# Output products of five FFN groups by a 2x2x2 Strassen scheme

## The chip, the cores and the metric

The kernel runs on one core of a Trainium2 chip. The core has a matrix engine (TensorE, PE in the profile), which multiplies a stationary operand of up to 128x128, loaded beforehand (PEld), with a moving operand of up to 512 columns and writes into PSUM; three engines for elementwise work (VectorE or DVE, ScalarE or ACT, GpSimd or POOL); and SyncE (SP), which in this kernel only issues DMAs. Each engine runs its own instructions in order, and semaphores order them between engines. The metric is the device time of one execution in microseconds (us), as the median of several runs.

## The reference, cut to what matters

```python
f = 1.0 / (1.0 + np.exp(-f_logit))                       # (4, 8, 768, 48): batch, head, time, feature
for t in range(S):
    state = f[:, :, t, :, None] * state + np.einsum('bhd,bhe->bhde', k[:, :, t], v[:, :, t])
    y[:, :, t] = np.einsum('bhd,bhde->bhe', q[:, :, t], state)
x = y.transpose(0, 2, 1, 3).reshape(3072, 384)
h = np.maximum(np.maximum(x @ w1, x @ w2), x @ w3)       # w1, w2, w3: (384, 768)
out = h @ w_out                                          # w_out: (768, 384)
```

A gated linear recurrence per head makes 3072 token rows of 384 features. A maxout FFN takes them to 768 and back to 384. Everything is float32 (the weights arrive as 64-bit floats and are converted on the chip).

## The kernel before, in words

The 3072 tokens are cut into 24 tiles of 128 (`NU`, index `u`: two batches by 64 time steps). Four tiles are one FFN group of `TOK` = 512 tokens (`GRP` = 4), so there are six groups, numbered g = 0 to 5 in the code.

*Attention.* For each tile, `sigmoids`, `scan`, `after`, `before` and `carry` prepare gates, decayed keys `kh`, decayed queries `qh` and the carried state; from the ninth tile on, `kh` (L328), `qh` (L339) and the carried `state` (L345) are GpSimd's. `pairs` (L380) multiplies keys with queries, `values` (L399, with `sums`, L424) applies the result to v and makes the new state, and `finish` (L470) adds what the state gives. ACT then copies y to the tile `heads` (L476, three copies). `pack` (L491) moves `heads` into `xT`, the transposed input of the FFN group, by ten DMAs: the eight heads have 48 rows each, and two of them cross a border between rows of 128. `pack(0, 2)` moves three tiles of a group together, `pack(3, 3)` the fourth. All ten are issued on SP, except at the very end, where SP and ACT take five each.

*FFN.* The first group runs `ffn_first`. During it, w1 is subtracted from w2 and w3 (`apart`), w1 is transposed (`turn`) and multiplied with w_out (`linear`); the product `w_lin` (384x384) lies in w1's place. With it the later groups use max(x w1, x w2, x w3) = x w1 + max(0, x(w2 - w1), x(w3 - w1)): `ffn(g, xT)` makes, for each of the six blocks `j` of 128 hidden rows, two products of 512 tokens (`product`, L511, three matmuls each, one for each `kt` of the 128-row blocks of `xT`). ACT applies Relu to the first (L612), VectorE takes the maximum with the second and writes `hm[:, j, :]` (L614). Then `outputs` makes one token tile of 128 at a time: three matmuls with `w_lin` (L528) and six with `w_out` (L532), all of 384 columns, into one PSUM buffer `p`; ACT copies it to `o` (L537), and `store` DMAs (L542) write two halves of 64 rows.

*The order.* It is written out by hand. The FFN is a queue of generators (`pending`), and each `yield` reports the nominal time of the matmuls just issued, `COLUMN` = 4/2.4 ns for each column. `fill(ns)` pulls parts from the queue until their reported time has used up `ns`; what is used too much or too little is carried on. From u = 4 on, every tile does: fill, `finish(u - 1)` and the packs, `pairs(u)`, loads and the next tile's sigmoids and scan, fill, `after` and `before` of the next tile, fill, `values(u)`, fill, loads, fill: five fills of `PART` = 2740 ns. `pack(3, 3)` and the start of the next `ffn` are both at the tiles u = 8, 12, 16, 20, and after the loop for the last group. What the group before has left in the queue at that point is issued before the next group's products.

*Buffers.* PSUM: two `p` buffers (`ps_f`), two `tr` buffers (`ps_tr`: transposes of the first eight tiles and the range test at the end), one each for `a` and `y`. In SBUF the weights are loaded as 64-bit words into `raw` buffers (12 of them). From u = 9 on they are loaded a second time, two pieces for each tile (`check_load`, L258), and ACT tests their range (`check_range`, L267 to L270). `o` has three buffers and serves the first tiles' x as well.

Of the kernel before, what the change touches and what calls it, by code (L numbers as in the profile page):

```python
# [9 lines left out]
FP32 = mybir.dt.float32  # L10
I32 = mybir.dt.int32
U32 = mybir.dt.uint32
AF = mybir.ActivationFunctionType
ALU = mybir.AluOpType
# [32 lines left out]
C = 64  # L47
# [8 lines left out]
def kernel(  # L56
# [12 lines left out]
    nc = tc.nc  # L69
# [3 lines left out]
    UT = 2 * C  # L73
# [16 lines left out]
    def fast():  # L90
        ctx = ExitStack()
        with ctx:
# [100 lines left out]
            pieces = [(w_in[i][:, :, j * 128:(j + 1) * 128], src[:, j * 128:(j + 1) * 128])  # L193
                      for j in range(NJ) for i, src in enumerate((moe_w1, moe_w2, moe_w3))]
            pieces += [(w_out[:, j:j + 1, :], moe_w_out[j * 128:(j + 1) * 128, :]) for j in range(NJ)]
            RAW = 12
            PIECE = NK * 128
            raw, raw_next = {}, []

            def load_weights(count, done=0, queue=nc.sync):  # L200

                for n in range(len(raw_next), min(len(raw_next) + count, done + RAW, len(pieces))):
                    raw_next.append(n)
                    dst, src = pieces[n]
                    a = dst.shape[1]
                    if src.dtype != FP32:
                        raw[n] = work.tile([128, 2 * PIECE], U32, name="raw", bufs=RAW)
                        dst, src = raw[n].rearrange("p (a c) -> p a c", a=a), src.bitcast(U32)
                    queue.dma_start(out=dst, in_=src.rearrange("(a p) c -> p a c", a=a))

# [42 lines left out]
            def check_load(n):  # L253
                src = pieces[n][1]
                if src.dtype != FP32:
                    raw[n] = work.tile([128, 2 * PIECE], U32, name="raw", bufs=RAW)
                    a = pieces[n][0].shape[1]
                    nc.sync.dma_start(out=raw[n].rearrange("p (a c) -> p a c", a=a),  # L258
                                      in_=src.bitcast(U32).rearrange("(a p) c -> p a c", a=a))
# [173 lines left out]

            heads = keep.tile([128, HP, TOK], FP32, name="heads")

            def y_by_tokens(u):

                d = ready[u]
                y = d["y"]
                if u >= 2:  # L440

                    new = states[u % 2][:, 0, 0:1]
                    nc.tensor.matmul(ps_f.tile([1, 1], FP32, name="p"), lhsT=new, rhs=new, start=True, stop=True)
                    st = d["state"].rearrange("p (a h) d -> p a h d", a=2)
                    for hp in range(HP):
                        for par, a in FOUR:
                            r = slice(par * DP, par * DP + D)
                            nc.tensor.matmul(y[a * C:(a + 1) * C, par, hp * D:(hp + 1) * D], lhsT=d["qh"][r, a, hp, :],
                                             rhs=st[r, a, hp, :], start=False, stop=(hp == HP - 1), skip_group_check=True)
                x = work.tile([UT, DM], FP32, name="o", bufs=3)  # L450
                nc.scalar.copy(x.rearrange("t (hp par d) -> t par hp d", hp=HP, par=2),
                               y[:, :, 0:HP * D].rearrange("t par (hp d) -> t par hp d", d=D))
                d["x"] = x
# [67 lines left out]
            def new_top(w):  # L521
                return work.tile([128, TOK], FP32, name="top")[:, 0:w]

            def outputs(g, hm, i, xT=None):
                p = ps_f.tile([128, TOK], FP32, name="p")
                if g:
                    for kt in range(NK):
                        nc.tensor.matmul(p[:, 0:DM], lhsT=xT[:, kt, i * UT:(i + 1) * UT], rhs=w_lin[:, kt, :],  # L528
                                         start=(kt == 0), stop=False)
                    yield NK * DM * COLUMN  # L530
                for j in range(NJ):
                    nc.tensor.matmul(p[:, 0:DM], lhsT=hm[:, j, i * UT:(i + 1) * UT], rhs=w_out[:, j, :],  # L532
                                     start=(g == 0 and j == 0), stop=(j == NJ - 1))
                    if j == NJ // 2 - 1:
                        yield NJ // 2 * DM * COLUMN
                o = work.tile([UT, DM], FP32, name="o", bufs=3)
                nc.scalar.copy(o, p[:, 0:DM])  # L537
                c, bp = divmod(g * GRP + i, 2)
                for a in range(2):
                    t0 = (2 * bp + a) * S + c * C  # L540
                    last = g * GRP + i == NU - 1 and a
                    (nc.scalar if last else nc.sync).dma_start(out=out[t0:t0 + C, :], in_=o[a * C:(a + 1) * C, :])  # L542
                yield NJ // 2 * DM * COLUMN

            def apart(j):

# [25 lines left out]
            def ffn_first(xT):  # L572
                hm = new_hm()
                steps = [(j, slice(n * HALF, (n + 1) * HALF)) for n in range(2) for j in range(J_HALF)]
                steps += [(j, slice(0, TOK)) for j in range(J_HALF, NJ)]
                done, n_step = 1, 0
                for j, t in steps:
                    w = t.stop - t.start
                    for i in range(3):
                        p = yield from product(0, xT, j, i, t)  # L580
                        if i == 0:
                            top = new_top(w)
                            nc.scalar.copy(top, p)
                        else:
                            nc.vector.tensor_tensor(hm[:, j, t] if i == 2 else top, p, top, op=ALU.max)
                        n_step += 1
                        ahead = n_step + 1 if n_step <= 6 else 7 + (n_step - 6) * 5 // 6 if n_step <= 12 else 12 + (n_step - 12) * 6 // 5
                        for r in range(done, min(ahead, len(pieces))):
                            if r + 2 < len(pieces):
                                round_begin(r + 2)  # L590
                            if r + 1 < len(pieces):
                                round_end(r + 1)
                            done = r + 1
                        load_weights(2, done)
                        yield (1 if w == TOK else NK) * w * COLUMN
                for i in range(GRP):
                    for j in range(i * NJ // GRP, (i + 1) * NJ // GRP):
                        apart(j)
                    yield from outputs(0, hm, i)
                    for j in range(i * NJ // GRP, (i + 1) * NJ // GRP):  # L600
                        yield from turn(j)
                for a in range(NK):
                    yield from linear(a)

            def ffn(g, xT):
                hm = new_hm()
                for j in range(NJ):
                    for i in (1, 2):
# [3 lines left out]
                            nc.scalar.activation(top, p, AF.Relu)  # L612
                        else:
                            nc.vector.tensor_tensor(hm[:, j, :], p, top, op=ALU.max)  # L614
                        yield TOK * COLUMN
                for i in range(GRP):
                    yield from outputs(g, hm, i, xT)

            pending = []

# [423 lines left out]
```

## Time and profile before

| what | value |
|---|---|
| median of 3 runs | 457.15 us (457.14 to 458.05) |
| the profiled execution, its own time | 457.98 us |
| its span from first to last instruction | 456.2 us |
| TensorE matmuls of the products, L511 | 504 records, 212.8 us busy |
| of the outputs, L532 and L528 | 288 and 120 records, 99.3 and 42.4 us busy |
| VectorE maximum `hm`, L614, 128x512 | 30, mean 681 ns |
| ACT copy `o`, L537, 128x384 | 24, mean 477 ns |
| GpSimd `kh`, `qh`, `state` (L328, L339, L345) | mean 1960, 1176, 857 ns |
| DMA `raw` (384 KB), `xT` (24 KB), `out` (96 KB) | 5.5, 1.9, 2.2 us from issue to landing |

How to read it: the span is one execution as the hardware profiler saw it, on one core. Busy time is the union of an engine's instructions. A float32 matmul shows as two records, one for each pass, and each has its own weight load. The recorded duration of a matmul includes the way through the pipeline, so records overlap: the spacing of their starts is what counts. The timeline merges neighbouring records of a kind and gives their number (x6), and in brackets how long the engine had been idle and who ended that. A line marked SPq or ACTq is the issuing of DMAs on that queue.

### The profile page before, as it was taken

What the parts mean: (1) busy time and instruction counts of PE and PEld (TensorE: products, weight loads), DVE (VectorE), ACT (ScalarE), POOL (GpSimd) and SP (SyncE); (2) the same over time, 40 slices, a digit from 0 to 9 for tenths busy, and PEclk for the clock granted to TensorE, in tenths of its full rate; (3) what the DMA queues carried; (4) which work ended last, traced back from release to release, by engine and by line L of the source; (5) the groups of instructions that cost most, each with busy time, mean ns of one, the idle gap of its engine ahead of it and who ended that gap; (6) DMA issues with size and microseconds to landing.
All of it is one profiled execution on the core that took longest, in us unless ns stands there. A gap on an engine that the chain in (4) does not pass through costs nothing.

```text
span 456.2 us, 10209 instructions
## 1 busy us (share of the span) xinstructions
PE 432.9 (95%) x4062; PEld 244.1 (54%) x4062; DVE 253.4 (56%) x510; ACT 150.1 (33%) x350; POOL 103.9 (23%) x125
## 2 busy tenths in 40 slices
PE   4989999999999999999999999999989999999995
PEld 3777655556554456554456654455544455544553
DVE  6976757556858569357779557759456520011100
ACT  2434757403312214414414524504324331111000
POOL 2153654403033033032033023023032120000000
PEclk9999999999999999999999999999999999999999
DMA  8889997202547733647763557643746003100011
GB/s 169 213 245 299 259 205 89 36 19 71 94 66 88 133 93 72 147 78 146 92 164 77 147 104 131 98 142 72 165 78 124 2 0 88 45 9 0 4 35 37
DMA packets 177140, 47.13 MB, mean 103 GB/s; under 512 B 154816, under 2 KB 175552, under 8 KB 177088
## 3 DMA queue, kind: packets, MB, share of 16 engines
q1 hardware_dynamic: 173616, 45.64, 47.6%
q10 hardware_dynamic: 3472, 0.79, 0.8%
q8 instruction: 33, 0.54, 0.5%
q14 instruction: 19, 0.16, 0.1%
HBM read 37.75 MB, written 4.72 MB: 93 GB/s over the span
## 4 chain that ended last, share of the span: by engine, by line
PE 84%; DVE 5%; ACT 4%; DMA 4%; issue 2%; SPq 1%; POOL 0%; ACTq 0%; DVEq 0%
PE p L511 42%; PE p L532 18%; PE p L528 7%; PE y L470 3%; PE p L565 3%; PE y L399 2%; PE y L424 2%; PE a L380 2%; DVE r L317 2%; DMA raw<-in_moe_w_out_dram 2%; ACT heads L476 1%; PE tr L279 1%; DMA xT<-heads 1%; ACT sig L299 1%; PE y L395 1%
## 5 line engine op out<-in xcount | busy, mean ns | idle before, releaser
L511 PE MATMUL p<-xT,w_in 128*128 128x512 f32 (+1 forms) x504 | 212.8, 569 | 7.5 <-ACT top L612 2.8
L511 PEld LDWEIGHTS p<-xT,w_in 128*128 128x128 f32 x504 | 92.0, 190 | 104.2 <-issue 85.2
L532 PE MATMUL p<-w_out,hm 128*128 128x384 f32 x288 | 99.3, 491 | 1.3 <-ACT w_in L558 1.0
L532 PEld LDWEIGHTS p<-w_out,hm 128*128 128x128 f32 x288 | 53.6, 190 | 37.1 <-ACT w_in L558 1.3
L370 DVE STREAM_TRANSPOSE ks<-kh 32x128 f32<-32x128 f32 x224 | 67.7, 302 | 3.5
L614 DVE TENSOR_TENSOR hm<-p,top 128x512 f32<-128x512 f32 x30 | 20.4, 681 | 80.9 <-PE p L511 80.5
L327 POOL COPY ends<-r 128x8 f32<-128x8 f32 x24 | 6.7, 279 | 187.0 <-DVE r L317 187.0
L612 ACT ACTIVATE top<-p 128x512 f32<-128x512 f32 x30 | 17.8, 594 | 91.9 <-PE p L511 91.9
L383 DVE TENSOR_TENSOR at<-a,mask 128x512 f32<-128x512 f32 x24 | 16.6, 692 | 48.8 <-PE a L380 48.8
L528 PE MATMUL p<-w_in,xT 128*128 128x384 f32 x120 | 42.4, 489 | 0.0
L537 ACT COPY o<-p 128x384 f32<-128x384 f32 x24 | 11.4, 477 | 93.6 <-PE p L532 90.1
L476 ACT COPY heads<-y 64x256 f32<-64x256 f32 (+1 forms) x60 | 22.1, 369 | 54.9 <-PE y L470 45.5
L328 POOL TENSOR_TENSOR kh<-kt,r 128x512 f32<-128x512 f32 x16 | 31.4, 1960 | 35.4 <-DVE kt L284 33.2
L317 DVE TENSOR_TENSOR_SCAN r<-gate,from_one 128x520 f32<-128x520 f32 x24 | 29.8, 1241 | 6.6 <-ACT gate L296 3.4
L528 PEld LDWEIGHTS p<-w_in,xT 128*128 128x128 f32 x120 | 22.5, 190 | 16.0 <-issue 1.9
L335 DVE TENSOR_TENSOR_SCAN prod<-gate,from_inv 128x520 f32<-128x520 f32 x24 | 30.2, 1257 | 0.0
L247 POOL TENSOR_TENSOR w_in<-top_bits,rest_bits 128x384 uint32<-128x384 uint32 x18 | 20.8, 1161 | 26.6 <-DVE top_bits L241 12.1
L339 POOL TENSOR_TENSOR qh<-qt,prod 128x512 f32<-128x512 f32 x16 | 18.8, 1176 | 6.2 <-DVE qt L284 6.2
L345 POOL TENSOR_TENSOR state<-st,ends 128x384 f32<-128x384 f32 x22 | 18.9, 857 | 0.2
L399 PEld LDWEIGHTS y<-at,v_ld 64*64 64x64 f32 x640 | 11.2, 134 | 13.0 <-issue 6.1
L380 PE MATMUL a<-qh,kh 48*64 48x64 f32 x768 | 15.7, 219 | 1.0 <-DVE qh L339 0.8
L470 PEld LDWEIGHTS y<-qh,state 48*48 48x48 f32 x640 | 10.3, 119 | 11.7 <-issue 11.7
(101 smaller groups left out, 366.3 us busy)
## 6 DMA issues: line engine op xcount, KB each, us to landing
raw<-in_moe_w_dram SPq DMA_DIRECT2D x36, 384.0 KB, 5.5
v_ld<-in_v_dram SPq DMA_DIRECT2D x48, 96.0 KB, 3.1
raw<-in_moe_w_out_dram SPq DMA_DIRECT2D x12, 384.0 KB, 4.9
out_dram<-o SPq DMA_DIRECT2D x47, 96.0 KB, 2.2
xT<-heads SPq DMA_DIRECT2D x30, 72.0 KB, 2.2
f_ld<-in_f_logit_dram SPq DMA_DIRECT2D x32, 64.0 KB, 2.7
k_ld<-in_k_dram SPq DMA_DIRECT2D x32, 64.0 KB, 2.7
q_ld<-in_q_dram SPq DMA_DIRECT2D x32, 64.0 KB, 2.9
```

The costliest lines, as they stand in the source:

```text
L247: nc.gpsimd.tensor_tensor(dst, by(top), by(rest), op=ALU.add)
L317: nc.vector.tensor_tensor_scan(r[:, 0:LEN][:, ::-1], flat(gate)[:, ::-1], flat(from_one)[:, ::-1], 1.0, op0=ALU.mult, op1=ALU.max)
L328: (nc.vector if u < BY_ROWS else nc.gpsimd).tensor_tensor(kh.rearrange("p h a t -> p a h t"), kt, by_batch(r[:, 1:LEN + 1].rearrange("p (x ...
L335: nc.vector.tensor_tensor_scan(flat(prod), flat(gate_tiles[u % 2]), flat(from_inv[u % 2]), 1.0, op0=ALU.mult, op1=ALU.max)
L370: nc.vector.transpose(ks[n * 32:(n + 1) * 32, :, par, e0:e0 + 32], kh[p0:p0 + 32, :, a, t0:t0 + 32])
L380: nc.tensor.matmul(p[t, par, hp * C:(hp + 1) * C], lhsT=kh[r, hp, a, :], rhs=qh[r, a, hp, :], start=True, stop=True)
L470: nc.tensor.matmul(y[o:o + D, a, hp * C:(hp + 1) * C], lhsT=st[r, a, hp, :], rhs=d["qh"][r, a, hp, :], start=False, stop=(hp == HP - 1), s ...
L476: nc.scalar.copy(heads[o, :, t0 + a * C:t0 + (a + 1) * C], y[i, a, 0:HP * C].rearrange("p (h t) -> p h t", h=HP))
L511: nc.tensor.matmul(p if g or w < TOK else p.rearrange("p (two t) -> p two t", two=2), lhsT=w_in[i][:, kt, j * 128:(j + 1) * 128], rhs=rhs, ...
L528: nc.tensor.matmul(p[:, 0:DM], lhsT=xT[:, kt, i * UT:(i + 1) * UT], rhs=w_lin[:, kt, :], start=(kt == 0), stop=False)
L532: nc.tensor.matmul(p[:, 0:DM], lhsT=hm[:, j, i * UT:(i + 1) * UT], rhs=w_out[:, j, :], start=(g == 0 and j == 0), stop=(j == NJ - 1))
L614: nc.vector.tensor_tensor(hm[:, j, :], p, top, op=ALU.max)
```

## The change

In the groups g = 1 to 5 the outputs are made for two token tiles at once. A pair's hidden rows form a 2x2 block matrix A (two token tiles by two halves of the 768 hidden rows), `w_out` a 2x2 block matrix of halves of the rows and halves of the 384 columns. Strassen's scheme, in Winograd's form, makes the product of two such matrices with seven block products for eight. Here four sums of blocks of A (`s1` to `s4`) are made for each pair, on GpSimd, and four of w_out once, on VectorE (`mix`, during the products of the group g = 1, one for each j; one replaces its corner of `w_out`). The three matmuls of `w_lin` for each half of the columns are added into the same sums where the scheme lets them: four uses for a pair, one of them with a difference of `w_lin`'s halves (`mixed["x"]`, the fifth `mix`). Each block product is three matmuls of 192 columns, 33 for a pair. They go to four banks of PSUM, the two `p` and the two `tr` buffers. ACT copies the first bank (`e`), VectorE makes five sums of 128x192 out of PSUM and GpSimd two more, and after the last matmuls of the pair both tiles are stored, with four DMAs.

The buffers follow: 11 raw buffers, six of which (`raw_kept`) hold the mixed weights and the sums once the weights are converted, so that the second loading has five; two `o` buffers of two tiles each instead of three of one.

```diff
-            RAW = 12
+            RAW, RAW_KEPT = 11, 6
+
+            def new_raw(kept=False):
+                return work.tile([128, 2 * PIECE], U32, name="raw_kept" if kept else "raw",
+                                 bufs=RAW_KEPT if kept else RAW - RAW_KEPT)
...
                     if src.dtype != FP32:
-                        raw[n] = work.tile([128, 2 * PIECE], U32, name="raw", bufs=RAW)
+                        raw[n] = new_raw(n % RAW >= RAW - RAW_KEPT)
...
                 if src.dtype != FP32:
-                    raw[n] = work.tile([128, 2 * PIECE], U32, name="raw", bufs=RAW)
+                    raw[n] = new_raw()
...
+            def new_o():
+                return work.tile([UT, 2, DM], FP32, name="o", bufs=2)
...
-                x = work.tile([UT, DM], FP32, name="o", bufs=3)
+                x = new_o()[:, 0]
...
-            def outputs(g, hm, i, xT=None):
+            def store(u, o):
+                c, bp = divmod(u, 2)
+                for a in range(2):
+                    t0 = (2 * bp + a) * S + c * C
+                    last = u == NU - 1 and a
+                    (nc.scalar if last else nc.sync).dma_start(out=out[t0:t0 + C, :], in_=o[a * C:(a + 1) * C, :])
+
+            def outputs(hm, i):
                 p = ps_f.tile([128, TOK], FP32, name="p")
-                if g:
-                    for kt in range(NK):
-                        nc.tensor.matmul(p[:, 0:DM], lhsT=xT[:, kt, i * UT:(i + 1) * UT], rhs=w_lin[:, kt, :],
-                                         start=(kt == 0), stop=False)
-                    yield NK * DM * COLUMN
                 for j in range(NJ):
                     nc.tensor.matmul(p[:, 0:DM], lhsT=hm[:, j, i * UT:(i + 1) * UT], rhs=w_out[:, j, :],
-                                     start=(g == 0 and j == 0), stop=(j == NJ - 1))
+                                     start=(j == 0), stop=(j == NJ - 1))
                     if j == NJ // 2 - 1:
                         yield NJ // 2 * DM * COLUMN
-                o = work.tile([UT, DM], FP32, name="o", bufs=3)
+                o = new_o()[:, 0]
                 nc.scalar.copy(o, p[:, 0:DM])
-                c, bp = divmod(g * GRP + i, 2)
-                for a in range(2):
-                    t0 = (2 * bp + a) * S + c * C
-                    last = g * GRP + i == NU - 1 and a
-                    (nc.scalar if last else nc.sync).dma_start(out=out[t0:t0 + C, :], in_=o[a * C:(a + 1) * C, :])
+                store(i, o)
                 yield NJ // 2 * DM * COLUMN
+
+            mixed = {}
+            HJ, HD = NJ // 2, DM // 2
+            corner = lambda k, n: w_out[:, k * HJ:(k + 1) * HJ, n * HD:(n + 1) * HD]
+
+            def new_mix(cols):
+                return new_raw(True).bitcast(FP32).rearrange("p (a c) -> p a c", c=cols)
+
+            def mix(n):
+
+                if n == 0:
+                    mixed.update({i: new_mix(2 * PIECE // 4)[:, 0:HJ, :] for i in (2, 3, 4, "x")})
+                    mixed.update({"s": [new_mix(128) for _ in range(2)], 1: corner(0, 1)})
+                dst, x, y = ((mixed[3], corner(1, 1), corner(0, 1)), (mixed[1], corner(0, 1), corner(0, 0)),
+                             (mixed[2], corner(1, 1), mixed[1]), (mixed[4], corner(1, 0), mixed[2]),
+                             (mixed["x"], w_lin[:, :, 0:HD], w_lin[:, :, HD:DM]))[n]
+                nc.vector.tensor_tensor(dst, x, y, op=ALU.subtract)
+
+            def outputs_pair(g, hm, i, xT):
+
+                A = lambda n, k: hm[:, k * HJ:(k + 1) * HJ, (i + n) * UT:(i + n + 1) * UT]
+                X = lambda n: xT[:, :, (i + n) * UT:(i + n + 1) * UT]
+                sums_of = lambda n: mixed["s"][n // 2][:, n % 2 * HJ:(n % 2 + 1) * HJ, :]
+                s1, s2, s3, s4 = (sums_of(n) for n in range(4))
+                for dst, x, y, op in ((s3, A(0, 0), A(1, 0), ALU.subtract), (s1, A(1, 0), A(1, 1), ALU.add),
+                                      (s2, s1, A(0, 0), ALU.subtract), (s4, A(0, 1), s2, ALU.subtract)):
+                    nc.gpsimd.tensor_tensor(dst, x, y, op=op)
+                banks = [ps.tile([128, TOK], FP32, name=nm) for ps, nm in ((ps_f, "p"), (ps_tr, "tr")) * 2]
+                cols = lambda n: slice(n * HD, (n + 1) * HD)
+
+                def into(bank, n, *terms):
+                    terms = [(lhs[:, k], rhs[:, k]) for lhs, rhs in terms for k in range(3)]
+                    for m, (lhs, rhs) in enumerate(terms):
+                        nc.tensor.matmul(banks[bank][:, cols(n)], lhsT=lhs, rhs=rhs, start=(m == 0),
+                                         stop=(m == len(terms) - 1))
+                    return len(terms) * HD * COLUMN
+
+                o = new_o()
+                e = work.tile([128, PIECE], FP32, name="rest_bits", bufs=3)
+                t = work.tile([128, PIECE], FP32, name="top_bits", bufs=4)
+                plus = lambda engine, dst, x, y: engine.tensor_tensor(dst, x, y, op=ALU.add)
+                yield into(0, 0, (A(0, 0), corner(0, 0)))
+                yield into(1, 0, (X(0), w_lin[:, :, cols(0)]), (A(0, 1), corner(1, 0)))
+                yield into(2, 0, (X(1), mixed["x"]), (A(1, 1), mixed[4]))
+                yield into(3, 0, (X(1), w_lin[:, :, cols(1)]), (s3, mixed[3]))
+                cost = into(0, 1, (s1, mixed[1]))
+                nc.scalar.copy(e, banks[0][:, 0:DM])
+                yield cost
+                cost = into(1, 1, (s2, mixed[2]))
+                plus(nc.vector, t[:, cols(0)], banks[1][:, cols(1)], e[:, cols(0)])
+                plus(nc.vector, o[:, 0, cols(0)], banks[1][:, cols(0)], e[:, cols(0)])
+                yield cost
+                cost = into(3, 1, (X(0), w_lin[:, :, cols(1)]), (s4, corner(1, 1)))
+                plus(nc.vector, t[:, cols(1)], banks[3][:, cols(0)], t[:, cols(0)])
+                plus(nc.vector, o[:, 0, cols(1)], banks[3][:, cols(1)], t[:, cols(0)])
+                plus(nc.vector, o[:, 1, cols(0)], banks[2][:, cols(0)], t[:, cols(1)])
+                plus(nc.gpsimd, o[:, 0, cols(1)], o[:, 0, cols(1)], e[:, cols(1)])
+                plus(nc.gpsimd, o[:, 1, cols(1)], t[:, cols(1)], e[:, cols(1)])
+                for n in range(2):
+                    store(g * GRP + i + n, o[:, n])
+                yield cost
...
-                    yield from outputs(0, hm, i)
+                    yield from outputs(hm, i)
...
@@ -612,9 +678,11 @@
                             nc.scalar.activation(top, p, AF.Relu)
                         else:
                             nc.vector.tensor_tensor(hm[:, j, :], p, top, op=ALU.max)
+                        if g == 1 and i == 1 and j < 5:
+                            mix(j)
                         yield TOK * COLUMN
-                for i in range(GRP):
-                    yield from outputs(g, hm, i, xT)
+                for i in range(0, GRP, 2):
+                    yield from outputs_pair(g, hm, i, xT)
```

## The prediction

> **What bounds the kernel now.** I read the page's busy shares and slices first, then the chain of waits, then the timeline around each handover between two FFN groups.
>
> ```profile
> PE 432.9 (95%) x4062; PEld 244.1 (54%) x4062; DVE 253.4 (56%) x510; ACT 150.1 (33%) x350; POOL 103.9 (23%) x125
> PE   4989999999999999999999999999989999999995
> PE 84%; DVE 5%; ACT 4%; DMA 4%; issue 2%; SPq 1%; POOL 0%; ACTq 0%; DVEq 0%
> ```
>
> TensorE is busy 95% of the span and carries 84% of the chain; one slice after the start is below 9 tenths. So work taken from TensorE shortens the kernel, provided TensorE finds other work at that place. The end is matmuls without a gap (chain of waits, 425 us to the end; start, us, what):
>
> ```profile
> 428.07 1.94 PE p L528 x6
> 430.01 3.87 PE p L532 x12
> 451.37 0.48 ACT o L537
> ```
>
> Six records of 384 columns take 1.94 us, 322.7 ns each; a fp32 matmul is two records. The 54 records of 512 columns at 396.64 last 23.34 us, the last one's pipeline drain (0.17) included: 429.1 ns each. Slope 0.831 ns a column.
>
> Now the handovers. The 512-token xT of an FFN group is complete only after pack(3, 3), whose ten DMAs follow the third token tile's L470 and L476. Timeline of before at the fourth of them (u = 20), then at the last one:
>
> ```profile
> 323.36 0.66 PE L470 MATMUL y<-qh,state 48*48 48x64 f32 x32
> 324.11 1.14 ACT L476 COPY heads<-y 128x256 f32<-128x256 f32 x3 [0.17 <-PE y L470]
> 324.42 2.20 PE L528 MATMUL p<-w_in,xT 128*128 128x384 f32 x6
> 326.46 4.03 PE L532 MATMUL p<-w_out,hm 128*128 128x384 f32 x12
> 326.77 6.79 SPq L491 DMA_DIRECT2D xT<-heads  x10
> 330.42 0.69 PE L399 MATMUL y<-at,v_ld 64*64 64x64 f32 x32
> 331.50 1.12 PE L511 MATMUL p<-xT,w_in 128*128 128x512 f32 x2
> 334.47 1.52 PE L511 MATMUL p<-xT,w_in 128*128 128x512 f32 x3 [1.84 <-DMA xT<-heads]
> ...
> 390.14 0.66 PE L470 MATMUL y<-qh,state 48*48 48x64 f32 x32
> 391.95 3.59 SPq L491 DMA_DIRECT2D xT<-heads  x5
> 392.04 3.21 ACTq L491 DMA_DIRECT2D xT<-heads  x5
> 392.77 4.03 PE L532 MATMUL p<-w_out,hm 128*128 128x384 f32 x12
> 396.64 1.02 PE L511 MATMUL p<-xT,w_in 128*128 128x512 f32 x2
> ```
>
> The reader is to see what covers the copies: nine output matmuls left over from the group before (6 + 12 records, 5.8 us). The ten issues on SP alone take 6.8 us. At u = 20 the cover falls 1.84 us short; at the end it just suffices, the issues being split over two queues.
>
> **What the Trainium skill says.** (1) "TensorE: Matmul & The Clock Gate", section "LDWEIGHTS (loading the stationary operand)": a load takes the columns over 1.2, 107 ns for 128. The profile shows 190 ns for one. The matmuls of 192 columns should take 163 ns, so it matters which of the two binds. The timeline of before, transposes of 128 columns with 140 ns a load:
>
> ```profile
> 11.61 0.42 PEld L279 LDWEIGHTS p<-ident,q_ld 128*128 128x128 f32 x4
> 11.61 0.66 PE L279 MATMUL p<-ident,q_ld 128*128 128x128 f32 x4
> 12.10 0.60 PE L279 MATMUL tr<-ident,f_ld 128*128 128x128 f32 x4
> ```
>
> Four of these pairs start every 0.49 us, 0.12 each, less than the 0.14 of one recorded load: part of a load's duration is latency and overlaps the next. The trace agrees with the page's reading. (2) Same page, "HAM oscillation — how this bites in real kernels": TensorE falls back to half its clock after idling over about 3.4 us. The trace of before has no such gap after the start. It does show the slow clock at the start: the transposes at 5.12 to 7.71 start 0.86 us apart per four, against 0.49 later. (3) "SBUF — State Buffer", "SBUF: two separate sides": a VectorE instruction with two SBUF inputs and a GpSimd instruction exclude each other. No row of before isolates that.
>
> **The change part by part.**
>
> *Matmuls.* Before, a pair of token tiles takes 18 matmuls of 384 columns: 36 x 322.7 ns = 11.62 us. After: 33 matmuls of 192 columns. By the slope a record takes 322.7 - 192 x 0.831 = 163 ns, so 66 x 163 = 10.77 us. Saved 0.85 a pair, ten pairs: -8.5 us. If the recorded load bound (190 + 2.7), a pair would take 12.7 us: +10.9. Below 163 nothing speaks.
>
> *The planner's account.* Each part still reports columns x 1.667 ns, so each group brings 1.9 us less to the fills, which stay 5 x 2740 ns per token tile. The left-over work at each handover shrinks from group to group. In the changed program's order on TensorE, what stands between the L470 of the third tile and the first product of the next group is: u = 12, pairs, 18 half matmuls and the values matmuls; u = 16, pairs and 12 half matmuls; u = 20, pairs alone; at the end nothing. Times below count from the end of L470 (T).
>
> *u = 12.* The first product comes at T + 0.66 + 18 x 0.326 + 1.35 = T + 7.9. In before the copies start at T + 0.85 (189.35 against 188.5), 0.65 apart, and land in about 2.4. Rows kt = 0, 1, 2 (issues 3, 7, 10) are there at T + 4.6, 7.2, 9.1, needed at 7.9, 8.8, 9.6. No stall.
>
> *u = 16.* First product at T + 0.66 + 3.9 = T + 4.6, kt = 1 needed at 5.4, there at 7.2: stall +1.8.
>
> *u = 20.* Here a pair ends right before L470, and its four stores (before: two) stand ahead of the copies on SP. They wait for the pair's last sums: three VectorE sums of 192 columns, 0.36 each by the rows of 512 (681 ns) and 256 (423), then two GpSimd sums, about 0.45 each (half the 0.88 below). The first store can start 1.35 after the last matmul, T + 0.7; four issues of 0.62: the copies start at T + 3.2 (before: T + 2.75). Rows there at T + 6.7, 9.3, 11.3. TensorE has only pairs (0.66) and three matmuls (2.6) up to T + 12.1: idle 8.9, before 1.84: +7.0.
>
> *End.* Same stores ahead on SP, copies from T + 3.2 on SP and T + 1.3 on ACT, landing 2.0: kt = 0 at T + 5.8, kt = 1 at 7.1, kt = 2 at 7.7. TensorE has nothing else: delay 6.2, before 0: +6.2.
>
> *Tail.* ACT's copy (0.48) and two parallel stores become VectorE 3 x 0.36, GpSimd 2 x 0.45, and three stores one after another on SP, 0.62 each. Last issue at 2.6 after the last matmul, before 0.6: +2.0.
>
> *Clock.* Idle stretches of about 6 us at u = 20 and at the end exceed the 3.4 of the skill. If the clock falls, some 3.4 us run at half rate each time, losing about 2. Bounds 0 and +4; I take one of them, +2.0.
>
> *Sums on GpSimd.* Four of 128x384 a pair: `L345` of that size takes 857 ns, `L339` scaled from 512 gives 882; 0.88 x 4 + 0.9 = 4.4 us a pair, 44 in all on an engine busy 104. Within a pair the first sum is used after 18 matmuls (5.9 us), the last after 27. In the second pair they queue behind the first pair's two closing sums, done 2.2 after its end: first sum ready at 3.1, last at 5.7. Covered with 3 us to spare; GpSimd's kh and qh (1.96 + 1.18) standing between would use that up and cost up to 0.5 a pair. Those two are delayed by up to 4 us in turn; three fills of 2.7 lie before their use in L380. I take 0; bounds 0 and +5, which also holds the exclusion by the skill's third point.
>
> *VectorE, ACT, buffers.* VectorE gets 5 x 0.36 a pair and five differences of weights once (about 0.7 each), at 56% busy; ACT loses one copy a pair. Two o buffers of double size for three, 11 raw buffers for 12: a weight is asked for one step later, and its landing takes 5.5 against ten steps of over 2 us: 0. PSUM: a pair holds both p buffers and both tr buffers; tr has no other user after the eighth tile, and each is drained at least 9 half matmuls before its next use: 0. The check loads have 5 buffers, each free two half-steps before it is asked for: 0.
>
> Sum: -8.5 + 1.8 + 7.0 + 6.2 + 2.0 + 2.0 = +10.5 on the profiled execution's 457.98 (span 456.2 and 1.8 around it): 468.5. The median of the runs, 457.15, is 0.8 lower: 467.6.
>
> **The rivals.**
>
> *A, faster: the saving stays.* If the copies are there when TensorE wants them, or the order leaves it other work, only 8.5 - 2.0 is left, some 451; with half of the handover cost (7.5) 458. For it: TensorE is the bound and idles only 13 us today. Against it: ten SP issues take 6.8 us whatever TensorE does, and nothing stands before the product at u = 20 and at the end. It decides when all the handovers together cost under 6.5.
>
> *B, slower still: the load binds.* 192-column matmuls at the 190 ns of the recorded load: +10.9 for -8.5, so 467.6 + 19.4 = 487. Against it: the transposes.
>
> *C: sums come late.* GpSimd or VectorE hold TensorE up within pairs, 0.5 a pair over the forecast, both clock drops besides: 467.6 + 5 + 2 = 475.
>
> *D: the change does less.* The stalls come but the clock stays, and landings are 1 us quicker each time: 467.6 - 2 - 3 = 462.6. I count it with the forecast.
>
> **How the numbers follow.** What a measurement can tell here from no change is 0.2%, 0.9 us. Forecast (with D) 0.74, own range 461 to 472; A 0.11, of which 0.02 within 0.2%; B 0.05; C 0.10. Faster 0.09, same 0.02, slower 0.89. Range for 8 in 10: 459 (leaving most of A out) to 473 (B and half of C out).
>
> **What would show it.** Six records of 192 columns in 0.98 us confirm the matmul step; 1.15 would be B. At the handover to the fifth and to the last group the page should show TensorE waiting for DMA xT, 5 us or more in one piece each, small or none at u = 12. After such a gap records of 512 columns 0.86 apart show the clock. Last store issued 2.6 after the last matmul. Waits of TensorE for POOL before the matmuls of `into` would be C. A total of such DMA waits under 7 us makes the prediction wrong.

## The result, and the profile after

The changed kernel takes 470.38 us (median of 4 runs, 469.83 to 470.9) against 457.19 us of the kernel before in the same comparison: ratio 1.0284, 95% interval 1.0264 to 1.0304. It is slower by 13 us. The profiled execution took 470.9 us, its span is 469.2 us, 13.0 more than before.

The page of the changed kernel, busy shares, slices and the chain by engine:

```profile
PE 432.1 (92%) x4362; PEld 286.7 (61%) x4362; DVE 272.1 (58%) x565; ACT 145.4 (31%) x340; POOL 155.9 (33%) x185
...
PE   4989999999998999999999899999499999499994
PEclk9989999999999999999999899999689999799998
...
PE 62%; SPq 4%; ACT 3%; DVE 3%; DMA 2%; issue 1%; POOL 0%; ACTq 0%; DVEq 0%; POOLq 0%
```

TensorE's busy time has not fallen (432.9 before), though each pair has fewer matmul columns. Two slices at 4 tenths are new, the 29th and the 35th, and under them the granted clock (PEclk, the share of full speed at which TensorE was let run) falls to 6 and 7 tenths. The chain leaves TensorE more often, and for SP's queue.

First the matmuls themselves. The timeline of the changed kernel, the last pair of all:

```profile
451.52 1.14 PE L582 MATMUL p<-w_out,hm 128*128 128x192 f32 x6
...
452.49 1.14 PE L582 MATMUL tr<-w_in,xT 128*128 128x192 f32 x6
...
461.27 1.14 PE L582 MATMUL tr<-w_out,raw_kept 128*128 128x192 f32 x6
```

Six records of 192 columns start every 0.97 us, 162 ns each. From the first to the last group of six there are ten steps, and with the last one's 0.97 the pair takes 451.52 to 462.24 = 10.72 us; before it took 11.62. The arithmetic does save 0.9 us a pair, 9.0 in all.

Now the handovers. The timeline of the changed kernel at u = 20:

```profile
329.09 0.66 PE L477 MATMUL y<-qh,state 48*48 48x64 f32 x32
...
329.82 1.14 ACT L483 COPY heads<-y 128x256 f32<-128x256 f32 x3 [3.07 <-DVE o L589]
...
330.56 2.71 SPq L536 DMA_DIRECT2D out_dram<-o  x4
...
333.37 6.28 SPq L498 DMA_DIRECT2D xT<-heads  x10
...
336.82 2.05 PE L518 MATMUL p<-xT,w_in 128*128 128x512 f32 x2 [6.60 <-DMA xT<-heads]
...
339.12 3.01 PE L518 MATMUL p<-xT,w_in 128*128 128x512 f32 x3 [0.25 <-DMA xT<-heads]
```

Where nine output matmuls covered the copies before, only the pairs matmuls (0.65 us at 329.57) are left. The heads are ready at 330.96, but SP first issues four stores (2.7 us), and the first three copies, which TensorE needs for its first row of xT, come behind them. It stands 6.60 us, then 0.25. And the two records at 336.82 last 2.05 us: the clock is at half. The same view at the end:

```profile
400.98 0.66 PE L477 MATMUL y<-qh,state 48*48 48x64 f32 x32
...
402.46 2.67 SPq L536 DMA_DIRECT2D out_dram<-o  x4
402.88 3.22 ACTq L498 DMA_DIRECT2D xT<-heads  x5
405.22 3.09 SPq L498 DMA_DIRECT2D xT<-heads  x5
...
407.74 2.90 PE L518 MATMUL p<-xT,w_in 128*128 128x512 f32 x3 [6.10 <-DMA xT<-heads]
```

At u = 16 the wait is 2.00 us (261.17 to 263.17), at u = 12 there is none. Timeline of the changed kernel at u = 16, where TensorE's matmuls of L477 end at 256.60:

```profile
256.40 2.23 SPq L262 DMA_DIRECT2D raw<-in_moe_w_dram  x2
...
258.73 5.66 SPq L498 DMA_DIRECT2D xT<-heads  x9
...
263.17 1.10 PE L518 MATMUL p<-xT,w_in 128*128 128x512 f32 x2 [2.00 <-DMA xT<-heads]
```

Here two loads of `raw` stand ahead of the copies on SP until 258.63. The list of waits puts all four waits (2.00, 6.60, 0.25 and 6.10) under one row, so it holds nothing else:

```profile
PE p L518 <- DMA xT<-heads: 15.0, 4, 6.6
```

The clock is seen when the span is cut at its changes (windows of the changed kernel: from:to, length, busy time and instructions of PE, PEld, DVE, ACT, POOL, then the granted clock, DMA share and GB/s):

```profile
32.30:35.70 3.40, 3.40 (x12) 2.64 (x11) 1.81 (x6) 0.48 (x1) 0.28 (x1) 0.50 0.75 134
264.40:267.80 3.40, 3.40 (x56) 1.90 (x58) 1.47 (x2) 0.00 (x0) 3.40 (x3) 0.50 0.31 61
332.70:342.90 10.20, 5.82 (x7) 1.97 (x8) 5.11 (x10) 0.62 (x3) 4.13 (x4) 0.50 0.31 68
404.40:411.20 6.80, 3.46 (x4) 1.46 (x5) 0.00 (x0) 0.00 (x0) 0.00 (x0) 0.50 0.32 71
```

Four stretches run at 0.50, whole multiples of 3.41 us; the execution of the kernel before shows 1.00 in the same windows. TensorE is busy in them for 3.40 + 3.40 + 5.82 + 3.46 = 16.1 us, so at most half of that, 8.0 us, is lost. This is why TensorE's busy time did not fall: it does less at half speed.

Last the tail, from the last matmul to the end of the span, timeline of the changed kernel:

```profile
463.20 0.59 POOL L589 TENSOR_TENSOR o<-o,rest_bits 128x192 f32<-128x192 f32 x1 [5.51 <-DVE o L589]
463.75 0.59 POOL L589 TENSOR_TENSOR o<-top_bits,rest_bits 128x192 f32<-128x192 f32 x1
463.81 2.01 SPq L536 DMA_DIRECT2D out_dram<-o  x3
```

The last matmul ends at 462.41, the span 6.8 us later; before it was 4.9.

So the span's 13.0: matmuls -9.0; waits for xT +2.0 (u = 16), +5.0 (u = 20: 6.85 against 1.84), +6.1 (end); tail +1.9. That makes +6.0. The remaining 7.0 are left for the clock, inside its bound of 8.0; this is what is left over and not a measurement.

### The profile page after: what moved, and what is told of

It reads as the page before. It is cut to its first block, busy times and chain, and to the rows that moved or that the text cites. A ratio compares the mean times of both kernels' runs of the same rounds, so it can differ in the third digit from the quotient of the medians.

```text
span 469.2 us, 10977 instructions
## 1 busy us (share of the span) xinstructions
PE 432.1 (92%) x4362; PEld 286.7 (61%) x4362; DVE 272.1 (58%) x565; ACT 145.4 (31%) x340; POOL 155.9 (33%) x185
## 4 chain that ended last, share of the span: by engine, by line
PE 62%; SPq 4%; ACT 3%; DVE 3%; DMA 2%; issue 1%; POOL 0%; ACTq 0%; DVEq 0%; POOLq 0%
PE p L518 32%; PE tr L582 12%; PE p L582 8%; SPq L498 3%; PE y L403 2%; PE y L477 2%; PE p L541 2%; DMA xT<-heads 2%; PE y L428 1%; ACT heads L483 1%; PE a L384 1%; PE p L631 1%; ACT sig L303 1%; DVE r L321 1%; SPq L183 1%
## 5 line engine op out<-in xcount | busy, mean ns | idle before, releaser
L518 PE MATMUL p<-xT,w_in 128*128 128x512 f32 (+1 forms) x504 | 219.4, 584 | 19.5 <-DMA xT<-heads 15.0
L518 PEld LDWEIGHTS p<-xT,w_in 128*128 128x128 f32 x504 | 94.4, 195 | 118.8 <-issue 99.8
L582 PE MATMUL tr<-w_in,xT 128*128 128x192 f32 x180 | 34.8, 329 | 0.0
L575 POOL TENSOR_TENSOR raw_kept<-hm 128x384 f32<-128x384 f32 x20 | 20.0, 1013 | 42.8 <-DVE hm L680 28.4
L582 PEld LDWEIGHTS tr<-w_in,xT 128*128 128x128 f32 x180 | 29.7, 190 | 0.4
L589 DVE TENSOR_TENSOR top_bits<-tr,rest_bits 128x192 f32<-128x192 f32 x10 | 3.4, 344 | 37.5 <-PE tr L582 37.5
L582 PE MATMUL tr<-raw_kept 128*128 128x192 f32 x120 | 22.8, 326 | 0.0
L343 POOL TENSOR_TENSOR qh<-qt,prod 128x512 f32<-128x512 f32 x16 | 19.8, 1240 | 3.0 <-DVE qt L288 3.0
L582 PEld LDWEIGHTS tr<-raw_kept 128*128 128x128 f32 x120 | 20.0, 190 | 0.0
L349 POOL TENSOR_TENSOR state<-st,ends 128x384 f32<-128x384 f32 x22 | 18.8, 856 | 0.2
L595 ACT COPY rest_bits<-p 128x384 f32<-128x384 f32 x10 | 4.8, 475 | 43.5 <-PE p L582 43.4
```

The costliest lines, as they stand in the source:

```text
L343: (nc.vector if u < BY_ROWS else nc.gpsimd).tensor_tensor(qh, qt, by_batch(prod[:, :, 1:]), op=ALU.mult)
L518: nc.tensor.matmul(p if g or w < TOK else p.rearrange("p (two t) -> p two t", two=2), lhsT=w_in[i][:, kt, j * 128:(j + 1) * 128], rhs=rhs, ...
L575: nc.gpsimd.tensor_tensor(dst, x, y, op=op)
L582: nc.tensor.matmul(banks[bank][:, cols(n)], lhsT=lhs, rhs=rhs, start=(m == 0), stop=(m == len(terms) - 1))
```

## The experiments

The theory after the result: the saving of the matmuls is real, and it is overpaid at the handovers, because the work reported to the planner no longer leaves anything to cover the copies, and because the half clock follows the waits. The rivals: the scheme itself is dear (sums, banks, loads), or the copies are late for another reason. Each time is a median; the kernel before took 457.92 us beside e1 to e4, 458.59 beside e5 to e7, 457.53 beside e8 and e9.

| kernel | us | ratio to before, 95% interval |
|---|---|---|
| e1_account | 453.89 | 0.9906 (0.9882 to 0.9929) |
| e2_warm | 465.30 | 1.0172 (1.0123 to 1.0221) |
| e3_deplete | 469.07 | 1.0245 (1.0213 to 1.0276) |
| e4_part | 452.50 | 0.9872 (0.9845 to 0.9899) |
| e5_both | 488.03 | 1.0661 (1.0625 to 1.0697) |
| e6_tail | 453.06 | 0.9897 (0.9864 to 0.9931) |
| e7_all | 453.42 | 0.9892 (0.9868 to 0.9917) |
| e8_late | 464.81 | 1.0157 (1.0123 to 1.0192) |
| e9_sums_first | 449.25 | 0.9815 (0.9788 to 0.9842) |

### e1_account: the changed kernel, reporting what the old outputs reported

```diff
-                    return len(terms) * HD * COLUMN
+                    return len(terms) * HD * COLUMN * 36 / 33
```

> Changed kernel with one edit: each part of a pair reports 36/33 of its columns to the fills, so that a pair counts as much as 18 matmuls of 384 columns did and 18 half matmuls are left over at each handover, as nine whole ones were before. Theory H (handovers: the left-over work ran out, xT copies became bare, the clock fell in the gaps): the saving of 8.5 us on matmuls stays, the tail costs 1.9, the handovers wait as in the kernel before within 1 us: 452 us (450 to 454). Theory P (the pair itself costs: sums on GpSimd and VectorE, four stores at once, PSUM banks held): the account changes nothing of that, 465 or more.

Measured: 453.89 us, inside the expected 450 to 454, 16.5 less than the changed kernel and 0.9% under the kernel before. Nothing of the scheme is altered, only when its parts are issued. At u = 20 the timeline of e1_account has this:

```profile
322.72 6.29 SPq L498 DMA_DIRECT2D xT<-heads  x10
...
324.67 1.14 PE L582 MATMUL tr<-w_out,raw_kept 128*128 128x192 f32 x6
...
325.74 0.69 PE L403 MATMUL y<-at,v_ld 64*64 64x64 f32 x32
...
330.38 1.95 PE L518 MATMUL p<-xT,w_in 128*128 128x512 f32 x4 [0.81 <-DMA xT<-heads]
```

Half a pair now lies beside the copies, and the longest wait is 0.81. All waits for xT together are 1.8 us for 15.0. No half clock stands in this execution. The scheme is not dear; its place in the order was.

### e2_warm: matmuls in the waits that nobody reads

```diff
             def ffn(g, xT):
+                busy({3: 4, 4: 14, 5: 13}.get(g, 0))
```

> Changed kernel with dummy matmuls of 256 columns (4, 14 and 13 of them, 1.7, 6.0 and 5.6 us) ahead of the first products of the groups g = 3, 4 and 5, where TensorE otherwise idles. Their results are not used. If the clock falls because of these gaps and costs 1.7, 1.8 and 2.0 us beside them: 465 us (463 to 467), with no half clock after 260 us. If the half clock lies under waits that are there anyway: 470. Theory P expects 470 or more too.

Measured: 465.30 us, as expected; the ratio falls from 1.0284 to 1.0172, 5.1 us. The copies come no earlier (at u = 20 they start at 330.39, 3.9 us after the end of L477's matmuls, against 3.6), but the stretch from 329 to 345 us has the granted clock 1.00 (windows of e2_warm):

```profile
329.00:345.00 16.00, 13.38 (x102) 7.53 (x101) 7.99 (x17) 3.30 (x10) 4.12 (x4) 1.00 0.44 74
396.00:413.00 17.00, 16.63 (x86) 10.18 (x85) 1.60 (x5) 2.30 (x5) 1.14 (x2) 1.00 0.18 40
```

So the half clock cost about 5 us by itself. The edit does not touch the gap at 29 us, but this execution has no half clock there either (1.00 from 29 to 36 us); so up to 1.7 us of the 5 can belong to that stretch, and the rest to the handovers.

### e3_deplete: the old outputs with the new account

```diff
-                    yield NK * DM * COLUMN
+                    yield NK * DM * COLUMN * 33 / 36
...
-                        yield NJ // 2 * DM * COLUMN
+                        yield NJ // 2 * DM * COLUMN * (33 / 36 if g else 1)
...
-                yield NJ // 2 * DM * COLUMN
+                yield NJ // 2 * DM * COLUMN * (33 / 36 if g else 1)
```

> Kernel before with one edit: the outputs of the groups g = 1 to 5 report 33/36 of their columns to the fills. All matmuls, copies and stores stay those of before; only what is left over at the handovers is that of the changed kernel (nothing at u = 20 and at the end). Theory H: 457.2 + 12 of idling + 5 of half clock = 474 us (470 to 477), slower than the changed kernel. Theory P: 457 to 460.

Measured: 469.07, +11 us without any Strassen in the kernel, though less than the expected 470 to 477. Timeline of e3_deplete at u = 20:

```profile
328.18 2.44 SPq L542 DMA_DIRECT2D out_dram<-o  x4
...
330.72 6.28 SPq L491 DMA_DIRECT2D xT<-heads  x10
...
334.03 2.04 PE L511 MATMUL p<-xT,w_in 128*128 128x512 f32 x2 [4.00 <-DMA xT<-heads]
```

The wait is 4.00 and not 6.60: the stores start 2.2 us earlier, counted from the end of L470's or L477's matmuls, since each old tile stores when its own sum is done, while a pair stores at its end. Waits and half clock (here 333.3 to 340.1 and 405.0 to 408.4) cost the changed kernel some 20 us (13.1 and 7.0); 11 of them come with the account alone. The pair's late stores are a part of their own, which e8_late measures.

### e4_part: smaller fills on top of e1

```diff
+                    PART = 2740 if u < 2 * GRP else 2660
```

> As e1_account, and every fill from the ninth tile on is 80 ns shorter, so that 30 half matmuls or more (9.7 us) are left over at u = 16, 20 and 33 at the end. Theory H: the wait at u = 20 that the kernel before has (1.84 us) goes too: 450 us (448 to 452), 2 below e1_account. If e1_account is already bound by something else than the handovers: the same as e1_account.

Measured: 452.50, just above the expected 448 to 452. No wait for xT is left in the list of waits, but TensorE has a row there that the changed kernel lacks, for VectorE's maximum at the first pair of three groups:

```profile
PE tr L582 <- DVE hm L680: 1.9, 3, 0.6
```

The profiled execution has a span of 452.1, 4.0 under that of the kernel before. The parts are -9.0 for the matmuls, -1.8 for the wait at u = 20, +1.9 for the tail, +1.9 for this row and at most +1.7 for half clock from 31.5 to 34.9 us, together -5.3; 1.3 us stay unexplained.

### e5_both: the copies shared by two queues

```diff
-                            pack(3, 3, xT)
+                            pack(3, 3, xT, both)
```

> The changed kernel with one thing altered: at the handovers of FFN groups 2 to 5 the ten copies that fill xT are shared by SyncE's and ScalarE's queues, five each, instead of ten on SyncE. If SyncE's issuing of ten copies sets the idle at u=20, that idle falls from 6.85 us (6.60 and 0.25) to 4 to 4.5, the wait at u=16 goes for the most part, TensorE's half-clock stretches there get shorter or go, and the time is 466 to 467. If the transport of the copies or the four stores ahead of them set it, the idle stays above 6 us and the time at 470.

Both expectations failed: 488.03 us, 18 more than the changed kernel. SyncE's waits in e5_both (engine, line, waited for: us in total, times, longest) have rows that the changed kernel lacks:

```profile
SPq L183 <- DMA xT<-heads: 9.7, 2, 9.5
SPq L536 <- DMA xT<-heads: 9.0, 2, 6.1
SPq L164 <- DMA xT<-heads: 6.4, 1, 6.4
```

Stores and loads that have nothing to do with xT wait for its copies, 25.1 us in all. The instruction records tell why: each of these DMAs waits for the semaphore that it will raise itself, from eight that go round in the order of the program. A store waited from 338.1 for number 105, last taken by the first copy on ScalarE's queue, which was issued only at 342.41. Timeline of e5_both there:

```profile
342.41 3.25 ACTq L498 DMA_DIRECT2D xT<-heads  x5
...
344.21 1.82 SPq L536 DMA_DIRECT2D out_dram<-o  x3
345.71 0.63 ACT L303 ACTIVATE sig<-f_ld 128x512 f32<-128x512 f32 x1 [3.33 <-DMA xT<-heads]
...
349.73 3.10 SPq L498 DMA_DIRECT2D xT<-heads  x5
...
352.33 1.19 PE L518 MATMUL p<-xT,w_in 128*128 128x512 f32 x1 [10.70 <-DMA xT<-heads]
```

SyncE goes on at 344.21, when the first of ScalarE's copies has landed, and its own five copies start at 349.73. The sigmoids, behind ScalarE's five issues, come up to 3.3 us late besides. So this kernel does not tell whether ten issues on one queue set the wait; it shows that the second queue is not free.

### e8_late: the stores behind the copies

The question that e5_both left was put again by moving four stores and no copy:

```diff
-                for n in range(2):
-                    store(g * GRP + i + n, o[:, n])
+                late.extend((g * GRP + i + n, o[:, n]) for n in range(2))
+                if i == 0 or g == NU // GRP - 1:
+                    store_late()
...
             def ffn(g, xT):
+                store_late()
```

> The changed kernel with one thing altered: the four stores of the last pair before a handover are issued after the copies into xT and not ahead of them, at u=20 and at the end; which queue issues the copies stays. If the issuing of the stores on SyncE is part of the wait, as the prediction has it (2.7 us of stores from 330.56 to 333.37 ahead of ten copies), the idle at u=20 falls from 6.85 to about 4.2 us and that at the end from 6.1 to 3.5 to 4, the half-clock stretches get shorter, and the time is 463 to 466. If the last transport or the copies of heads alone set the wait, the idles stay and the time is 470.

Measured: 464.81, within the expected 463 to 466. Timeline of e8_late:

```profile
328.80 0.66 PE L477 MATMUL y<-qh,state 48*48 48x64 f32 x32
...
330.31 7.20 SPq L498 DMA_DIRECT2D xT<-heads  x10
...
334.46 2.04 PE L518 MATMUL p<-xT,w_in 128*128 128x512 f32 x2 [4.53 <-DMA xT<-heads]
...
336.97 3.09 PE L518 MATMUL p<-xT,w_in 128*128 128x512 f32 x3 [0.46 <-DMA xT<-heads]
```

The wait at u = 20 falls from 6.85 to 4.99, that at the end from 6.10 to 3.48, and the half clock at the end lasts 3.4 us instead of 6.8. The first was expected to fall further, to about 4.2. Four stores ahead of the copies, at each of the two places, were worth 4.5 us of waits together. The wait that stays is the copies' own issuing and landing.

### e6_tail and e9_sums_first: one sum after the last matmul

Both start from e4_part. In e6_tail the product that feeds only one sum comes last, and the second tile is stored before it; e9_sums_first also moves a product to the front. Both send half of the stores of the last two tiles, and not of the last alone, to ScalarE's queue:

```diff
+                banks[0], banks[2] = banks[2], banks[0]
...
+                yield into(3, 0, (X(1), w_lin[:, :, cols(1)]), (s3, mixed[3]))
+                yield into(1, 0, (X(0), w_lin[:, :, cols(0)]), (A(0, 1), corner(1, 0)))
                 yield into(0, 0, (A(0, 0), corner(0, 0)))
-                yield into(1, 0, (X(0), w_lin[:, :, cols(0)]), (A(0, 1), corner(1, 0)))
...
+                store(g * GRP + i + 1, o[:, 1])
+                yield cost
+                cost = into(0, 0, (X(0), w_lin[:, :, cols(1)]), (s4, corner(1, 1)))
+                plus(nc.vector, o[:, 0, cols(1)], banks[0][:, cols(0)], e[:, cols(1)])
+                store(g * GRP + i, o[:, 0])
```

> The Strassen kernel of e4_part (handover work kept back by fills) with the pair's last products ordered so that after the last matmul one VectorE sum and one half of a store remain, instead of three sums and their stores. If the 1.9 us by which the tail is longer than before are the sums of the scheme in sequence, the time from the last matmul to the end of the span falls from about 6.8 to about 5 us, and the time is 450.5 (449 to 452) against e4_part's 452.5. If the store's own latency sets the tail, it stays at 452.5. If the new order brings waits for banks or for GpSimd into the pairs, gaps of 0.2 us or more appear at each of ten pairs and it is 454 or more.

Measured for e6_tail: 453.06, no gain. The tail did fall, from 6.8 us to 4.9 (last matmul at 446.33, span 451.3). But the waits of TensorE in e6_tail have a row that took more than that:

```profile
PE tr L583 <- DVE hm L681: 4.8, 3, 1.6
```

A pair's first product now asked for the second half of the hidden rows right after the group's last product, before VectorE had made the maximum. In e4_part, as told, the row has 1.9 us.

> e6_tail with the block product of the sum s3 issued first in each pair instead of fourth, so that the product that needs the hidden rows of the second half comes a microsecond later. In e6_tail three waits of 1.6 us for the last maximum of VectorE stand at the first pair of a group. If they are what took e6_tail's gain of 1.8 us in the tail, they fall below 0.7 us each and the time is 450 to 451.5. If s3 comes late from GpSimd, the waits move to s3 and it is 453 or more.

Measured for e9_sums_first: 449.25, a little under the expected 450 to 451.5; the row is gone, and the kernel is faster than the kernel before by 1.85% (95% interval 1.6 to 2.1%). The last product's end in e9_sums_first:

```profile
440.44 1.14 PE L583 MATMUL p<-w_out,raw_kept 128*128 128x192 f32 x6
...
441.30 1.39 ACTq L536 DMA_DIRECT2D out_dram<-o  x2
441.61 0.36 DVE L590 TENSOR_TENSOR o<-p,rest_bits 128x192 f32<-128x192 f32 x1 [0.34 <-PE p L583]
```

One sum of 0.36 us stands behind the last matmul. This is the fastest kernel of the study, 21 us under the changed one.

### e7_all: work in the gap at 29 us

```diff
                     if u == 2:
+                        busy(3)
```

> e6_tail with three more matmuls whose result nobody reads, put into TensorE's gap of 1.47 us at 29 us, where the half-clock stretch of 31 to 35 us begins in some executions. If the gap brings that stretch, no half clock shows there in the profile, the runs scatter by less than 1 us instead of 1.5 to 2, and the median is 449.5 to 450.5. If the stretch comes from something else (the load before it), it shows still in the profile or the scatter stays, and the time equals e6_tail's.

Measured: 453.42, the same as e6_tail and not the expected 449.5 to 450.5. Its profile has no half clock at 32 us, but e6_tail's has none either, with the gap of 1.47 us in it. Its four runs lie within 0.73 us and e6_tail's within 2.1; the smaller scatter was expected, but four runs are few. So this run does not show that filling the gap helps.

The traces themselves say more. In each execution all changes of the clock lie on one grid with steps of 3.413 us, and the grid lies elsewhere in each execution. Ten of the eleven profiled executions have the gap at 29 us (about 29.0 to 30.5). In six of them a border of the grid cuts it, and the clock stays full. In four one step of the grid holds it whole: half clock follows in the changed kernel, e4_part and e8_late, and not in e6_tail. One step of the grid each, in the changed kernel, in e6_tail and in the kernel before:

```profile
28.90:32.31 3.41, 1.94 (x74) 1.75 (x70) 1.88 (x5) 1.01 (x3) 0.99 (x1) 1.00 1.07 285
27.10:30.51 3.41, 1.95 (x41) 1.53 (x40) 3.13 (x6) 0.59 (x1) 2.07 (x2) 1.00 1.09 344
29.25:32.67 3.42, 2.06 (x70) 1.91 (x71) 1.88 (x4) 0.94 (x2) 1.00 (x1) 1.00 0.87 225
```

TensorE is idle for 1.47, 1.46 and 1.36 us of them, and half clock follows the first alone. So where the grid falls decides in part whether the gap brings half clock. Why e6_tail's step is followed by full clock stays open: idle time does not tell it from the first. What differs is the work beside the gap: matmuls with 128x128 weights fill 1.3 us of e6_tail's step and 0.1 to 0.7 us of the three that half clock follows; nearly all of the other busy time is matmuls with weights of 64x64 or less. Two steps with 1.73 us of idle time differ in the same way (e2_warm from 333.32, followed by full clock, 1.7 us; e5_both from 339.95, followed by half clock, 0.6 us). No run tests this.

## Why the prediction came out as it did

The forecast was 467.6 us, slower by waits at the handovers. The kernel came to 470.38, by these waits and by more half clock than forecast. That the totals lie within 3 us is luck in part: u = 20 cost 2 us less than forecast and the clock some 5 us more. Step by step:

| step | predicted, us | measured, us |
|---|---|---|
| matmuls | -8.5 (163 ns a record) | -9.0 (162 ns) |
| u = 12 | no stall | none |
| u = 16 | +1.8 (at the second row, copies from T + 0.85) | +2.0 (at the first row, copies from T + 2.1) |
| u = 20 | +7.0 (copies from T + 3.2) | +5.0 (copies from T + 3.6) |
| end | +6.2 | +6.1 |
| tail | +2.0 | +1.9 |
| clock | +2.0 (bounds 0 and 4) | about +7 left over (bound 8.0 from the windows); 5.1 by e2_warm |
| sums on GpSimd | 0 (bounds 0 and +5) | one wait of 0.43 |

*Matmuls.* Right, and for the reason given: the loads of 190 ns recorded do not bind, since six records start every 0.97 us. That fits the 107 ns for a load of 128 columns in the Trainium skill, "TensorE: Matmul & The Clock Gate", section "LDWEIGHTS (loading the stationary operand)", though no run here measures a load by itself. Rival B fell with it.

*The planner's account.* Shown by both sides: e1_account restores the account alone and is 16.5 us faster than the changed kernel; e3_deplete takes the account alone into the kernel before and loses 11 us.

*u = 16* came out right for another reason than the one given. The prediction let the copies start at T + 0.85 and had the second row come late. In the trace the loads of `raw` stand ahead of them on SyncE, the copies start at T + 2.1, and it is the first row that TensorE waits for.

*The clock* is the term that was mis-sized. The prediction expected two drops of 3.4 us, and took one of them. These two lasted 10.2 and 6.8 us. The execution has four, 23.9 us long together, and the other two follow idle times of 2.00 us (at u = 16) and 1.47 us (at 29 us), too short to matter by the prediction's 3.4 us. The gap at 29 us is there in the kernel before too, at full clock in its profiled execution, so it could have been listed as a possible drop but not as a sure one.

The section that was relied on, "HAM oscillation — how this bites in real kernels" of the same page of the Trainium skill, speaks of idling over about 3.4 us. Another section of it, "What's actually happening", says that the clock gate looks at windows of 3413 ns that run freely. The trace agrees with these windows: all stretches are multiples of 3.41 us, and those at 264.4, 332.7 and 404.4 begin 68, 88 and 109 steps of 3.413 us after the one at 32.3. The window before 264.4, 261.0 to 264.4, holds the whole wait of 2.00 us, while the kernel before keeps full clock after its wait of 1.84 us at u = 20 (332.63 to 334.47), which a border of its grid at 333.04 cuts. The trace does not agree with the first section's 3.4 us as a lower bound, nor with the table of the second, which has an idle window come before the half clock: the window before 264.4 was idle for 2.1 us of 3.41.

If all eleven profiled executions are cut by their own grids, half clock followed every window at full clock with 1.99 us or more of idle TensorE and none with 1.43 or less; from 1.47 to 1.80 both occur.

*u = 20* came out 2 us smaller. The prediction let TensorE use each row of xT at full speed and stand again for the next; at half clock its two records for the first row take 2.05 us and run while the second row lands, so that only 0.25 of waiting came after the first 6.60. Part of what the clock cost stood in place of a wait.

*Stores ahead of the copies* were named, with 2.5 us, and e8_late shows the step: waits fall by 4.5 us at the two places.

*Sums on GpSimd.* A sum of 128x384 takes 1.01 us for the estimated 0.88, a closing sum 0.59 for 0.45, and still nothing in a pair waits for them, but for one wait of 0.43 us for a VectorE sum at 320.66. Rival C did not come.

*Rival A*, that the saving stays, was put at 451 us. It is what the scheme gives when the handovers have cover: 452.50 in e4_part, whose order differs from the changed kernel's in its account and fills alone.

## What to carry to other kernels

Where an order is written with nominal costs, a step that becomes cheaper moves everything after it; look at what lay beside a transfer because of the old cost, and keep the account, or move cover there on purpose. Price a new wait of TensorE with the half clock that may follow it: here the waits cost 13 us and the clock another 5 to 7. And before a DMA is moved to another queue, list what stands behind it there and which DMAs share its semaphores.

## What the runs showed of the hardware that was not expected

- All changes of TensorE's clock in an execution lie on one grid of 3.413 us, which lies elsewhere in each execution. A wait of 2.00 us was followed by 3.41 us at half clock (264.4 to 267.8 of the changed kernel). A gap of 1.47 us was too where one step of the grid held it whole (32.3 to 35.7 of the changed kernel, 31.5 to 34.9 of e4_part), with one exception (e6_tail), and not where the grid cut it (the kernel before, e1_account).
- Splitting ten copies over two queues made this program 18 us slower, in large part because DMAs of one queue waited for the semaphores of the other's (e5_both: 25.1 us of such waits on SyncE).
- GpSimd's sums of 128x384 and 128x192 take 1013 and 587 ns, which gives 2.2 ns a column and some 160 ns besides. The shape alone does not set it: L349, also 128x384, takes 856 ns, and the estimate of 0.88 us rested on that operation.
